# Fewer bias copies, two more pairs of PSUM banks at the start, and unit 1's weights made ready inside attention

## The chip, the core and the metric

The kernel runs on one core of a Trainium2 chip. The time is the device time of one execution, in microseconds (us). The engines are TensorE (PE; its weight loads are listed as PEld), VectorE (DVE), ScalarE (ACT), GpSimd (POOL) and SyncE (SP), which here only starts DMAs. Each engine runs its instructions strictly in the order in which they were written.

## The reference, cut to what matters

```
rel   = i - j                                           # S = 576 positions
x     = log1p(|rel|) / log1p(max(i, 1))
bias  = relu(x @ w1 + b1) @ w2                          # 1 -> 32 -> 8 heads
s     = q @ k.T / 8 + bias                              # B = 2, H = 8, D = 64
attn  = softmax(s);  a = attn @ v                       # a: 1152 tokens x 512
p     = domain_probs / sum(domain_probs)                # 4 experts
out   = sum over e of p[:, e] * (relu(a @ w1[e]) @ w2[e])   # 512 -> 1024 -> 512
```

## The kernel before, in words

**Bias rows.** The bias is the same for both batches, and its 576 x 576 x 8 values are made in 36 "rows" n. A row needs four features (L283 on ACT or L285 on DVE, into a ring `fr` of 8), eight fp32 matmuls (`bias_mm`, L290) into a pair of PSUM banks, and one copy out by ACT (`bias_out`, L293) into `obr`, a ring of three buffers. From there DMAs spread the row over the partitions of the table `biasA` or `biasB` (`bias_dma`): rows 0 to 3 with four DMAs of 144 KB each (L301), the others with two (L306). Rows 0 to 3 are block 0, rows 4 to 11 block 1, and so on in eights; the blocks alternate between the two tables.

**Attention.** There are 9 tiles of 128 tokens, and in each 4 pairs of heads. Scores for one head take 4 or 8 matmuls (L318) into a pair of banks of the same pool `b2` that the bias rows use; `b2` has two entries, banks 0 to 3. `ttr` (L326, DVE) adds the bias and takes the maximum; it needs every row of its block landed. Then follow exp (L330, ACT), transposes (L335, PE, into banks 4 to 7, pool `b1`), their eviction (L339 on ACT or L341 on DVE), attn @ v (L350, PE), the normalisation (L354 to L367), and the split of the result into two fp16 parts (`xhi` L377, `xlo` L380). `v_max` (L257) reads each of the eight loads of v for a common scale.

**Experts.** Each expert is two units of half its hidden width; unit u is half u % 2 of expert u // 2. The weights of a unit come in four loads of 512 KB (`load_w`, L421; m = 0 is w1, m = 1 is w2, j the half). They are brought to a common scale: `wmax` (L427) on each load, `w_both` (L436), a round trip through HBM that spreads the maximum over the partitions (`w_send` L439, `w_cast` L443, `w_red` L446), `pow2` (L267 to L271); then they are split in two fp16 parts (`whi` L457 or L459, `wlo` L463; for w1, `w_split` L577 on ACT and L578 on DVE into `wn`). Unit 0 is computed directly: `mm1` (L475 to L477), `ev_a` (L480, L481, ACT), `ev_v` (L484, DVE, `hh`), `mm2` (L497 to L499), and `sum_up` (L504, later L506) into `acc`. Units 1 to 7 compute their first product from sums of blocks in seven instead of eight products (`prod`, L594), which needs sums of x (`x_whole` L547 on POOL, `x_sums` L544, `x_halves` L553) and of weights (`w_sums`, L574, POOL).

**What sets the order.** A planner (class `Plan`) lists all operations with their dependencies, pools, modelled cost (`COST`) and priority (`PR`, `PEN`), and writes an order for each engine when the kernel is built. `plan` covers attention, unit 0 and its weights; `plan_experts`, a second planner, follows it and covers units 1 to 7 and the rest of unit 0. In the kernel before, unit 1's four weight loads are issued between the two planners, and everything else on these weights belongs to the second.

Of the kernel before, what the change touches and what calls it, by code (L numbers as in the profile page):

```python
# [155 lines left out]
def tile_attention_moe(ctx: ExitStack, tc: tile.TileContext, qd, kd, vd, cst, ltab, dp, mw1, mw2, out):  # L156
    nc = tc.nc
    V, A, G, T, SP = nc.vector, nc.scalar, nc.gpsimd, nc.tensor, nc.sync
    PR = CFG["PR"]
# [436 lines left out]
    def plan_experts():  # L596
# [13 lines left out]
        def weights(u):  # L610
            at = 42.0 * u - 34 if u > 1 else 5.0
            p2, p1 = u - 2, u - 1
            for m in range(2):
                for j in range(2):
                    if u > 1:
                        after = [("part", p1, k) for k in range(4)] if m == 0 else [("whi", p1, j), ("wlo", p1, j)]
                        op(("load", u, m, j), "S", at - 10, 1.4, lambda m=m, j=j: load_w(u, m, j), deps=after)
                    prev = ([("gate", p2)] + all_("part", p2, 4) + [("wlo", p2, k) for k in range(2)]) if p2 >= 1 else []
                    op(("wmax", u, m, j), "V", at + 2 * m + j, 1.21, lambda m=m, j=j: wmax(u, m, j), deps=[("load", u, m, j)] if u > 1 else [], after=prev)
                op(("wboth", u, m), "V", at + 2 * m + 2, 0.16, lambda m=m: w_both(u, m), deps=[("wmax", u, m, j) for j in range(2)], after=[("wred", u - 1)] if u > 1 else [])  # L620
            op(("wsend", u), "S", at + 4, 0.1, lambda: w_send(u), deps=[("wboth", u, m) for m in range(2)])
            op(("wcast", u), "S", at + 4, 0.5, lambda: w_cast(u), deps=[("wsend", u)])
            op(("wred", u), "V", at + 5, 0.45, lambda: w_red(u), deps=[("wcast", u)])
            for m in range(2):
                op(("wscale", u, m), "V", at + 6, 0.75, lambda m=m: wscale(u, m), deps=[("wred", u)])
            op(("wsum", u), "G", at + 8, 5.9, lambda: w_sums(u), deps=[("wmax", u, 0, j) for j in range(2)], after=[("part", p1, k) for k in range(4)] if u > 1 else [])
            used = [("prod", p2, i, q, k) for i in range(2) for q in range(2) for k in range(7)] if p2 >= 1 else []
            for k, (c, fns) in enumerate(zip((1.15, 0.63, 0.63, 1.6), w_parts(u))):
                for e, x, fn in zip("AV", (0, 0.15 * c), fns):
                    op((("parth" if e == "A" else "part"), u, k), e, at + 12 + 3 * k, c + x, fn, deps=[("wscale", u, 0)] + ([("wsum", u)] if k != 1 else []) + ([("parth", u, k)] if e == "V" else []), after=used)  # L630
            for j in range(2):
                used2 = [("mm2", p2, tau) for tau in range(NTAU)] if p2 >= 0 else []
                op(("whi", u, j), "A", 42.0 * u - 12 + 4 * j, 1.14, lambda j=j: whi("A", u, 1, j), deps=[("wscale", u, 1)], after=used2)
                op(("wlo", u, j), "V", 42.0 * u - 11 + 4 * j, 1.28, lambda j=j: wlo("V", u, 1, j), deps=[("whi", u, j)])
            op(("gate", u), "V", 42.0 * u - 4, 0.29, lambda: gate_unit(u), deps=[("wscale", u, m) for m in range(2)], after=[("sum", p2, tau) for tau in range(NTAU)] if p2 >= 0 else [])

        def second(u, tau, at):
            i = tau // 5
            if u:
                deps = [("lo", u, i, k) for k in range(8)] + [("wlo", u, j) for j in range(2)]  # L640
# [106 lines left out]
    for n in range(36):  # L747
# [66 lines left out]
    with tc.manual_schedule():  # L814
# [78 lines left out]
```

## Time and profile before

| | |
|---|---|
| median of 3 runs | 575.23 us (573.58 to 576.18) |
| the profiled execution, whole | 574.98 us |
| its span in the profile | 573.2 us |
| PE busy | 547.8 us, 96% |
| DVE busy | 407.9 us, 71% |
| ACT busy | 296.7 us, 52% |
| POOL busy | 139.7 us, 24% |
| HBM read | 25.75 MB |

PE is busy in nearly all of the span, so what an edit can give is read from the few stretches in which PE stands still or runs at the lower clock. Busy times count the modelled ends of pipelined matmuls; a busy PE may still wait for its input between instructions that overlap.

### The profile page before, as it was taken

The page shows a single profiled execution, that of the slowest core. Times are in us where ns is not written, and L with a number is a line of the kernel's source. Part 1 is how long each engine was busy: PE and PEld are TensorE (multiplying, and loading weights), DVE is VectorE, ACT ScalarE, POOL GpSimd, SP SyncE. Part 2 cuts the span into 40 slices and gives each one's busy share as a digit, 9 for nine tenths or more (in the row PEclk, how much of TensorE's full clock was granted, in tenths as well). Part 3 has the DMA queues.
Part 4 walks back from the last instruction along what each step waited for, and adds up shares of the span by engine and source line. Part 5 has one row for each costly group of instructions (what it writes and reads, how often), then busy time and mean ns, then how long its engine had stood idle before and what let it go on. Part 6 is the DMA issues. An engine that isn't in the chain of part 4 may idle for free.

```text
span 573.2 us, 11028 instructions
## 1 busy us (share of the span) xinstructions
PE 547.8 (96%) x4354; PEld 342.9 (60%) x4354; DVE 407.9 (71%) x827; ACT 296.7 (52%) x616; POOL 139.7 (24%) x153
## 2 busy tenths in 40 slices
PE   8469999999999999969999999999999999999997
PEld 3125767677777864526655665665665665565753
DVE  7348888887887468988596895986868858544532
ACT  5357887887788741454344633625525435423410
POOL 0000000000000045005427352362453534312310
PEclk9567999999999999998999999999999999999999
DMA  5585252324323000023140031311412200000022
GB/s 182 176 276 168 66 172 65 96 87 116 85 73 138 2 1 1 2 36 120 10 148 11 21 127 11 109 40 10 148 10 74 74 9 1 2 1 1 1 74 91
DMA packets 22020, 40.63 MB, mean 71 GB/s; under 512 B 3024, under 2 KB 4048, under 8 KB 21968
## 3 DMA queue, kind: packets, MB, share of 16 engines
q1 hardware_dynamic: 21680, 39.33, 23.4%
q8 instruction: 34, 0.56, 0.4%
q10 hardware_dynamic: 288, 0.59, 0.3%
q14 instruction: 18, 0.15, 0.1%
HBM read 25.75 MB, written 2.37 MB: 49 GB/s over the span
## 4 chain that ended last, share of the span: by engine, by line
PE 86%; DVE 4%; DMA 3%; ACT 3%; issue 1%; SPq 1%; POOL 1%; ACTq 0%; DVEq 0%; POOLq 0%
PE bank L594 24%; PE bank L499 10%; PE bank L497 10%; PE bank L498 10%; PE bank L350 7%; PE bank L318 7%; PE bank L335 7%; PE bank L290 5%; DVE hh L484 2%; PE bank L361 2%; DMA vv<-vd 1%; DMA biasB<-obr 1%; PE bank L230 1%; SPq L301 1%; DMA biasA<-obr 1%
## 5 line engine op out<-in xcount | busy, mean ns | idle before, releaser
L594 PEld LDWEIGHTS <-wn 128*128 128x128 f16 x1176 | 115.6, 99 | 47.6 <-DVE wn L578 4.3
L674 POOL TENSOR_TENSOR hp<-hf,hp 128x320 f16<-128x320 f32 (+1 forms) x112 | 89.9, 818 | 201.0 <-ACT hf L673 198.7
L672 ACT ACTIVATE hp<-xsf 128x320 f16<-128x320 f32 (+1 forms) x112 | 49.0, 437 | 131.7 <-DVE xsf L662 131.4
L594 PE MATMUL bank<-xs,wn 128*128 128x320 f16 (+1 forms) x672 | 99.8, 289 | 3.4 <-DVE wn L578 2.0
L662 DVE SCALAR_TENSOR_TENSOR xsf<-bank,xsf 128x320 f32<-128x320 f32 (+1 forms) x196 | 82.3, 451 | 24.0 <-PE bank L594 17.1
L506 DVE SCALAR_TENSOR_TENSOR acc<-bank,gu,acc 128x512 f32<-128x512 f32 x63 | 47.1, 748 | 68.1 <-PE bank L499 68.0
L594 PE MATMUL bank<-xx,wn 128*128 128x320 f16 (+1 forms) x504 | 76.5, 288 | 2.3 <-DVE wn L578 1.6
L285 DVE TENSOR_SCALAR fr<-lt,npt 128x576 f32<-128x576 f32 x115 | 52.3, 515 | 13.0 <-PE bank L290 12.9
L330 ACT ACTIVATE er<-er,mr 128x576 f32<-128x576 f32 x72 | 55.1, 770 | 8.3 <-DVE mr L326 8.2
L499 PE MATMUL bank<-wb,hp 128*128 128x512 f16 x144 | 54.6, 379 | 1.1 <-POOL hp L674 1.1
L290 PE MATMUL bank<-fr,cs 128*32 128x288 f32 x576 | 46.9, 453 | 8.2 <-ACT obr L293 5.6
L497 PE MATMUL bank<-wb,hp 128*128 128x512 f16 x144 | 54.6, 379 | 0.0
L498 PE MATMUL bank<-wb,hp 128*128 128x512 f16 x144 | 54.6, 379 | 0.0
L318 PE MATMUL bank<-ks,qr 64*128 64x288 f32 (+1 forms) x320 | 48.6, 452 | 4.7 <-ACT obr L293 4.7
L673 ACT ACTIVATE hf<-xsf 128x320 f32<-128x320 f32 (+1 forms) x112 | 47.8, 427 | 0.0
L339 ACT ACTIVATE etr<-bank 128x512 f32<-128x512 f32 x71 | 38.2, 598 | 16.6 <-PE bank L335 14.3
L350 PE MATMUL bank<-etr,vv 128*64 128x128 f32 (+1 forms) x800 | 45.2, 265 | 0.0
L350 PEld LDWEIGHTS bank<-etr,vv 128*64 128x64 f32 x800 | 39.8, 137 | 8.6 <-issue 5.5
L499 PEld LDWEIGHTS <-hp 128*128 128x128 f16 x252 | 24.7, 98 | 31.2 <-POOL hp L674 1.5
L326 DVE CUSTOM_DVE_ANT_0 er<-bank,biasA 128x576 f32<-128x576 f32 x40 | 28.8, 755 | 19.8 <-PE bank L318 19.0
L335 PE MATMUL bank<-ident,er 128*128 128x128 f32 x324 | 42.3, 281 | 0.0
L335 PEld LDWEIGHTS bank<-ident,er 128*128 128x128 f32 x324 | 35.6, 143 | 10.8 <-issue 8.5
(103 smaller groups left out, 772.5 us busy)
## 6 DMA issues: line engine op xcount, KB each, us to landing
raw<-mw SPq DMA_DIRECT2D x32, 512.0 KB
biasA<-obr SPq DMA_DIRECT2D x48, 144.0 KB
biasB<-obr SPq DMA_DIRECT2D x32, 144.0 KB
vv<-vd SPq DMA_DIRECT2D x8, 320.0 KB
ks<-kd SPq DMA_DIRECT2D x8, 288.0 KB
qr<-qd SPq DMA_DIRECT2D x9, 256.0 KB
out<-acc SPq DMA_DIRECT2D x8, 256.0 KB
wg<-wd SPq DMA_DIRECT2D x7, 128.0 KB
```

Source lines behind the costliest of these rows:

```text
L285: ENG[e].tensor_scalar(out=f, in0=src, scalar1=npt[:, g:g + 1], scalar2=None, op0=ALU.max)
L290: T.matmul(buf["pb", n][32 * t:32 * t + 32, half, 0:288], W2, buf["f", n, t][:, 288 * half:288 * half + 288], start=True, stop=True)
L318: T.matmul(s_out(2 * p + h, c0, c1, half), q[r, c0:c1], ks[r, HP * b + hp, 288 * half:288 * half + 288], start=True, stop=True)
L330: A.activation(out=ehalf(u), in_=ehalf(u), func=AF.Exp, scale=-1.0, bias=buf["m", u // 2][:, u % 2:u % 2 + 1], accum_out=buf["sum", tau][: ...
L335: T.transpose(buf["t", tau, g][:, P * i:P * i + P], buf["e", HP * tau + hp][:, P * j:P * j + P], ident)
L350: T.matmul(x[64 * h:64 * h + 64, P * hp + c0:P * hp + c1], vv[:, HP * b + hp, 5 * h + i], buf["et", tau, g][:, P * j + c0:P * j + c1], sta ...
L497: T.matmul(ps, hh[:, ft, ts], wh[:, ft], start=(ft == 0), stop=False)
L498: T.matmul(ps, hh[:, ft, ts], wl[:, ft], start=False, stop=False)
L499: T.matmul(ps, hl[:, ft, ts], wh[:, ft], start=False, stop=(ft == 3))
L594: T.matmul(ps, w[lw][:, k], x[:, lx, k], start=k == 0 and lw + lx == 0, stop=k == 1 and lw == 1)
L662: V.scalar_tensor_tensor(out=tmp(name), in0=ps(a), scalar=2.0 ** -HS, in1=tmp(other), op0=ALU.mult, op1=ALU.add)
L674: op(("lo", u, i, x), "G", at + pos + EV, 0.2 + 0.6 * r, lambda: G.tensor_tensor(out=lo, in0=buf[f][:, 0:n], in1=hi, op=ALU.subtract), dep ...
```

## The change

**Copies of rows 0 to 3.** Each row now goes out in two DMAs of 16 x 8 x 576 values, which read all 128 partitions of the `obr` buffer and write 64 partitions of `biasA`. The bytes are the same.

**Banks.** Rows 0, 1, 4, 5, 6 and 7 (`EARLY`) take their PSUM banks from a new pool `b2s`, two pairs in banks 4 to 7. These are the banks of the transposes, so the first group of transposes now waits for the copies out of these six rows.

**Unit 1's weights.** Loads, `wmax`, `w_both`, round trip, `pow2`, `whi`, `wlo` and `gate_unit` of unit 1 are operations of the first planner, so that they stand inside the last part of attention; the second planner keeps only `w_sums` and `w_split` for unit 1. A part of the loads waits for `wlo`, since it uses the same buffers.

**Order.** All priorities, and `SWITCH`, are new numbers; two of the lines stand here.

```diff
-    SWITCH=16.97,
+    SWITCH=19.41,
-        scores=-30.04, ttr=-262.39, exp=64.6, tr=17.92, evict=47.99, av=20.65, recip=49.21, rmat=11.82,
+        scores=-303.4, ttr=-915.8, exp=113.09, tr=4.03, evict=36.16, av=7.58, recip=-125.93, rmat=3.25,
...
+    pools["b2s"] = [bank[:, 4 + 2 * i:6 + 2 * i] for i in range(2)]
...
-            dst = bias[0].rearrange("(z v a r) (h s) -> z r v a h s", z=2, v=2, a=8, r=4, h=H)
+            dst = bias[0].rearrange("(z a r) (h s) -> z r a h s", z=2, a=16, r=4, h=H)
             for z in range(2):
-                for v in range(2):
-                    SP.dma_start(out=dst[z, n, v], in_=buf["o", n][64 * v:64 * v + 64])
+                SP.dma_start(out=dst[z, n], in_=buf["o", n])
...
+    EARLY = (0, 1, 4, 5, 6, 7)
...   # bias_mm
-    new=[("b2", ("pb", n))]
+    new=[("b2s" if n in EARLY else "b2", ("pb", n))]
...   # tr, first group
+    deps = ... + ([] if tau or g else [("bias_out", n) for n in EARLY])
...
+    early = PR["wprep"] + 60
+    for m in range(2):
+        for j in range(2):
+            free = [("wlo", 1, 0), ("wlo", 1, 1)] if m == 0 else []
+            op("load1", (m, j), early, load_first, m, j, after=[("open_b",)] + free, new=[] if m else [("wr", ("wr1", j))])
+            op("wmax1", (m, j), early, wmax, 1, m, j, deps=[("load1", m, j)], use=[] if m else [("wr1", j)])
+            if m:
+                op("whi1", (j,), early, whi, 1, m, j, choice=True, deps=[("wscale1", m)])
+                op("wlo1", (j,), early, wlo, "V", 1, m, j, deps=[("whi1", j)])
+        op("both1", (m,), early, w_both, 1, m, deps=[("wmax1", m, j) for j in range(2)])
+        op("wscale1", (m,), early, wscale, 1, m, deps=[("wred1",)])
+    op("wsend1", (), early, w_send, 1, deps=[("both1", 0), ("both1", 1)])
+    op("wcast1", (), early, w_cast, 1, deps=[("wsend1",)])
+    op("wred1", (), early, w_red, 1, deps=[("wcast1",)])
+    op("gate1", (), early, gate_unit, 1, deps=[("wscale1", 0), ("wscale1", 1), ("prep_gate",)])
...   # after plan.emit(buf)
-        for m in range(2):
-            for j in range(2):
-                load_w(1, m, j)
```

The line numbers in the pieces of the order below are those of the kernel each piece is from; those after are higher by 1 to 25. Eight L290 (L291 after) are one bias row, eight L318 the scores of two heads at the start, L335 transposes, L350 attn @ v. On PE, from the start, before:

```order
L290 MATMUL bank<-fr,cs 32x288 x64
L318 MATMUL bank<-ks,qr 64x288 x8
L290 MATMUL bank<-fr,cs 32x288 x16
L335 MATMUL bank<-ident,er 128x128 x8
L318 MATMUL bank<-ks,qr 64x288 x8
L290 MATMUL bank<-fr,cs 32x288 x8
L318 MATMUL bank<-ks,qr 64x288 x8
L335 MATMUL bank<-ident,er 128x128 x8
```

On PE, the same place, after:

```order
L291 MATMUL bank<-fr,cs 32x288 x40
L318 MATMUL bank<-ks,qr 64x288 x8
L291 MATMUL bank<-fr,cs 32x288 x40
L335 MATMUL bank<-ident,er 128x128 x8
L318 MATMUL bank<-ks,qr 64x288 x8
L291 MATMUL bank<-fr,cs 32x288 x16
L335 MATMUL bank<-ident,er 128x128 x8
L318 MATMUL bank<-ks,qr 64x288 x8
```

The first scores stand behind five bias rows instead of eight; ten rows still stand ahead of the first transposes.

On SP, the DMAs from the first bias copies (L301) on; ks, vv, qr are the loads of k, v and q. Before:

```order
L301 DMA biasA<-obr 8x8x576 x16
L250 DMA ks<-kd 128x576
L306 DMA biasB<-obr 8x8x576 x2
L250 DMA ks<-kd 128x576 x2
L306 DMA biasB<-obr 8x8x576 x2
L250 DMA ks<-kd 128x576
L306 DMA biasB<-obr 8x8x576 x2
L253 DMA vv<-vd 128x640
L306 DMA biasB<-obr 8x8x576 x2
L253 DMA vv<-vd 128x640 x6
L306 DMA biasB<-obr 8x8x576 x4
```

On SP, the same place, after:

```order
L301 DMA biasA<-obr 16x8x576 x8
L251 DMA ks<-kd 128x576
L306 DMA biasB<-obr 8x8x576 x2
L251 DMA ks<-kd 128x576 x2
L306 DMA biasB<-obr 8x8x576 x4
L251 DMA ks<-kd 128x576
L306 DMA biasB<-obr 8x8x576 x2
L254 DMA vv<-vd 128x640 x2
L306 DMA biasB<-obr 8x8x576 x4
L254 DMA vv<-vd 128x640 x6
L306 DMA biasB<-obr 8x8x576 x4
L275 DMA qr<-qd 128x512 x3
```

All sixteen copies of block 1 (L306 into `biasB`) now stand ahead of the second load of q; before, the last four of them stood behind the next two loads of q.

On DVE, after the last token tile of attention (`xlo`); hh is the second half of unit 0's first product, raw and raw_1679 are weight buffers. Before:

```order
L484 TENSOR_TENSOR hh<-hf,hh 128x384 x8
L504 TENSOR_SCALAR acc<-bank,gu 128x512
L427 TENSOR_REDUCE ws<-raw 128x1 x2
L504 TENSOR_SCALAR acc<-bank,gu 128x512
L544 TENSOR_TENSOR xsf<-xsf 128x2x320
L436 TENSOR_TENSOR wx<-ws 128x1
L544 TENSOR_TENSOR xsf<-xsf 128x2x320
L504 TENSOR_SCALAR acc<-bank,gu 128x512
L544 TENSOR_TENSOR xsf<-xsf 128x2x320
L427 TENSOR_REDUCE ws<-raw_1679 128x1
```

On DVE, the same place, after (from the third hh on):

```order
L484 TENSOR_TENSOR hh<-hf,hh 128x384
L459 TENSOR_SCALAR wb<-raw_1669,ws 128x1024
L463 SCALAR_TENSOR_TENSOR wb<-raw_1669,ws,wb 128x1024
L484 TENSOR_TENSOR hh<-hf,hh 128x384
L463 SCALAR_TENSOR_TENSOR wb<-raw_1669,ws,wb 128x1024
L484 TENSOR_TENSOR hh<-hf,hh 128x384 x4
L504 TENSOR_SCALAR acc<-bank,gu 128x512
L578 SCALAR_TENSOR_TENSOR wn<-raw,ws,wn 128x512
L427 TENSOR_REDUCE ws<-raw_1669 128x1
L504 TENSOR_SCALAR acc<-bank,gu 128x512
L544 TENSOR_TENSOR xsf<-xsf 128x2x320
```

Unit 1's wmax are gone from here (in after all four stand ahead of the last `xlo`), its `whi` and `wlo` stand between the first hh, and a wmax of unit 2 has come in.

## Rows read from the trace of the kernel before

**Rows 1.** The page's 40 equal slices of the span: PE busy, and its clock, in tenths.

```profile
PE   8469999999999999969999999999999999999997
PEclk9567999999999999998999999999999999999999
```

**Rows 2.** Waits, 0 to 60 us: who waited for whom, us in total, times, longest.

```profile
ACT obr L293 <- DMA biasA<-obr: 9.3, 4, 3.1
PE bank L290 <- ACT obr L293: 5.6, 3, 2.6
PE bank L318 <- ACT obr L293: 4.7, 3, 2.4
```

**Rows 3.** ACT's timeline: start, us, operation, [idle before <- releaser].

```profile
27.96 0.74 ACT L293 ACTIVATE obr<-bank,cs 128x576 f32<-128x576 f32 x1 [3.12 <-DMA biasA<-obr]
...
31.36 0.74 ACT L293 ACTIVATE obr<-bank,cs 128x576 f32<-128x576 f32 x1 [2.00 <-DMA biasB<-obr]
```

**Rows 4.** PE's timeline, same columns, 32 to 58 us.

```profile
32.15 2.19 PE L318 MATMUL bank<-ks,qr 64*64 64x288 f32 x12 [2.17 <-ACT obr L293]
...
54.42 2.15 PE L290 MATMUL bank<-fr,cs 128*32 128x288 f32 x32
...
57.81 1.24 PE L318 MATMUL bank<-ks,qr 64*128 64x288 f32 x8
```

**Rows 5.** DVE's timeline: the first `ttr`, and the first one of block 1.

```profile
33.56 0.76 DVE L326 CUSTOM_DVE_ANT_0 er<-bank,biasA 128x576 f32<-128x576 f32 x1 [5.78 <-PE bank L318]
...
59.18 0.76 DVE L326 CUSTOM_DVE_ANT_0 er<-bank,biasB 128x576 f32<-128x576 f32 x1 [0.87 <-PE bank L318]
```

**Rows 6.** Stretches: busy of PE, PEld, DVE, ACT, POOL, then clock, DMA share, GB/s.

```profile
4.00:8.00 4.00, 4.00 (x18) 1.34 (x18) 3.79 (x16) 1.89 (x3) 0.00 (x0) 1.00 0.99 364
...
12.00:24.00 12.00, 6.64 (x60) 2.00 (x58) 5.24 (x13) 5.82 (x9) 0.00 (x0) 0.71 0.51 158
24.00:46.00 22.00, 14.46 (x118) 5.77 (x120) 10.85 (x24) 11.38 (x21) 0.00 (x0) 0.66 0.87 259
...
60.00:200.00 140.00, 140.00 (x1693) 103.95 (x1692) 111.00 (x276) 112.53 (x234) 3.42 (x4) 1.00 0.30 90
...
251.00:263.00 12.00, 7.32 (x32) 3.51 (x30) 10.15 (x13) 6.40 (x9) 0.79 (x1) 0.72 0.52 172
...
150.00:200.00 50.00, 50.00 (x572) 39.14 (x572) 35.49 (x90) 38.69 (x82) 0.68 (x1) 1.00 0.23 73
```

**Rows 7.** PE's timeline where unit 1's products begin.

```profile
252.15 0.45 PE L594 MATMUL bank<-xx,wn 128*128 128x320 f16 x2 [0.69 <-ACT wn L577]
...
257.76 1.25 PE L594 MATMUL bank<-xs,wn 128*128 128x320 f16 x4 [2.04 <-DVE wn L578]
```

**Rows 8.** SP's timeline (SPq is its DMA queue): DMAs issued, first 60 us.

```profile
9.56 13.54 SPq L301 DMA_DIRECT2D biasA<-obr  x16
...
43.14 1.13 SPq L274 DMA_DIRECT2D qr<-qd  x2
45.13 8.01 SPq L306 DMA_DIRECT2D biasB<-obr  x4
```

**Rows 9.** Groups of DVE instructions, 205.5 to 260 us: busy us, mean ns.

```profile
L504 DVE TENSOR_SCALAR acc<-bank,gu 128x512 f32<-128x512 f32 x9 | 6.7, 747 | 3.6 <-PE bank L499 3.6
L427 DVE TENSOR_REDUCE ws<-raw 128x1 f32<-128x1024 f32 x5 | 6.0, 1208 | 0.0
```

**Rows 10.** `whi` on DVE, whole span: ns min/median/max, when.

```profile
L459 DVE TENSOR_SCALAR wa<-raw,ws x1: 750/750/750, 120.1 to 120.1; 128x1024 f16<-128x1024 f32 x1
```

**Rows 11.** DVE's timeline, unit 0's second half and unit 2's first load.

```profile
209.02 11.71 DVE L484 TENSOR_TENSOR hh<-hf,hh 128x384 f16<-128x384 f32 x6 [1.02 <-ACT hh L481]
...
259.01 1.21 DVE L427 TENSOR_REDUCE ws<-raw 128x1 f32<-128x1024 f32 x1
```

**Rows 12.** POOL's timeline at the same time as the hh.

```profile
207.86 9.37 POOL L547 TENSOR_TENSOR xsf<-xx 128x2560 f32<-128x2560 f16 x2 [48.12 <-DVE xx L380]
```

**Rows 13.** SP's timeline: unit 2's loads.

```profile
255.34 3.96 SPq L421 DMA_DIRECT2D raw<-mw  x4
```

More of the change, by code (lines that the diff above doesn't have):

```diff
@@ L612, in weights @@
             p2, p1 = u - 2, u - 1
-            for m in range(2):
+            for m in range(2 if u > 1 else 0):
                 for j in range(2):
                     if u > 1:
-                        after = [("part", p1, k) for k in range(4)] if m == 0 else [("whi", p1, j), ("wlo", p1, j)]
+                        after = [("part", p1, k) for k in range(4)] if m == 0 else [("whi", p1, j), ("wlo", p1, j)] if p1 > 1 else []
                         op(("load", u, m, j), "S", at - 10, 1.4, lambda m=m, j=j: load_w(u, m, j), deps=after)
-                    prev = ([("gate", p2)] + all_("part", p2, 4) + [("wlo", p2, k) for k in range(2)]) if p2 >= 1 else []
+                    prev = (all_("part", p2, 4) + ([("gate", p2)] + [("wlo", p2, k) for k in range(2)] if p2 > 1 else [])) if p2 >= 1 else []
@@ L623, in weights @@
[L623 to L626, printed above, removed]
+                op(("wboth", u, m), "V", at + 2 * m + 2, 0.16, lambda m=m: w_both(u, m), deps=[("wmax", u, m, j) for j in range(2)], after=[("wred", u - 1)] if u > 2 else [])
@@ new lines, in weights @@
+            if u > 1:
+                op(("wsend", u), "S", at + 4, 0.1, lambda: w_send(u), deps=[("wboth", u, m) for m in range(2)])
+                op(("wcast", u), "S", at + 4, 0.5, lambda: w_cast(u), deps=[("wsend", u)])
+                op(("wred", u), "V", at + 5, 0.45, lambda: w_red(u), deps=[("wcast", u)])
+                for m in range(2):
+                    op(("wscale", u, m), "V", at + 6, 0.75, lambda m=m: wscale(u, m), deps=[("wred", u)])
+            op(("wsum", u), "G", at + 8, 5.9, lambda: w_sums(u), deps=[("wmax", u, 0, j) for j in range(2)] if u > 1 else [], after=[("part", p1, k) for k in range(4)] if u > 1 else [])
@@ L639, in second @@
             if u:
-                deps = [("lo", u, i, k) for k in range(8)] + [("wlo", u, j) for j in range(2)]
+                deps = [("lo", u, i, k) for k in range(8)] + ([("wlo", u, j) for j in range(2)] if u > 1 else [])
             else:
@@ L643, in second @@
             op(("mm2", u, tau), "T", at, 2.6, lambda: mm2(u, tau, buf["o", u, tau]), deps=deps, new=[("o", ("o", u, tau))])
-            op(("sum", u, tau), "V", at + 2.6 + EV, 0.75, lambda: sum_up(u, tau, buf["o", u, tau]), deps=[("mm2", u, tau)] + ([("gate", u)] if u else []), use=[("o", u, tau)], after=[("sum", u - 1, tau)] if u else [])
+            op(("sum", u, tau), "V", at + 2.6 + EV, 0.75, lambda: sum_up(u, tau, buf["o", u, tau]), deps=[("mm2", u, tau)] + ([("gate", u)] if u > 1 else []), use=[("o", u, tau)], after=[("sum", u - 1, tau)] if u else [])
             if u == NU - 1:
@@ L726, in plan_experts @@
         return plan
+    EARLY = (0, 1, 4, 5, 6, 7)
+    KIND = {"load1": "load_w", "wmax1": "wmax", "whi1": "whi", "wlo1": "wlo", "both1": "wmax_both", "wscale1": "wscale", "wsend1": "wsend", "wcast1": "wcast", "wred1": "wred", "gate1": "gate_unit"}
     def op(kind, key, prio, fn, *args, choice=False, **kw):
-        plan.add((kind,) + key, kind, prio, (lambda e: fn(e, *args)) if choice else (lambda e: fn(*args)), **kw)
+        name, kind = kind, KIND.get(kind, kind)
+        plan.add((name,) + key, kind, prio, (lambda e: fn(e, *args)) if choice else (lambda e: fn(*args)), **kw)
     def chain(kind, u):
@@ L755, in tile_attention_moe @@
         old = [("ttr", 16 * (block - 2) + 7)] if block > 1 else []
-        op("bias_mm", (n,), base + PR["bias_mm"], bias_mm, n, deps=[("feat", n, t) for t in range(4)], after=chain("bias_mm", n) + (old if (n - 4) % 8 >= 3 else []) + ([("scores", (n - 8) // 2 if n < 12 else n - 10)] if n >= 8 else []), new=[("b2", ("pb", n))], use=[("f", n, t) for t in range(4)], mode="col4")
+        op("bias_mm", (n,), base + PR["bias_mm"], bias_mm, n, deps=[("feat", n, t) for t in range(4)], after=chain("bias_mm", n) + (old if (n - 4) % 8 >= 3 else []) + ([("scores", (n - 8) // 2 if n < 12 else n - 10)] if n >= 8 else []), new=[("b2s" if n in EARLY else "b2", ("pb", n))], use=[("f", n, t) for t in range(4)], mode="col4")
         op("bias_out", (n,), base + PR["bias_out"], bias_out, n, deps=[("bias_mm", n)], after=chain("bias_out", n), new=[("ob", ("o", n))], use=[("pb", n)])
-        op("bias_dma", (n,), base + PR["bias_dma"], bias_dma, n, deps=[("bias_out", n)] + old, after=chain("bias_dma", n), use=[("o", n)], cost=COST["bias_dma8" if n < 4 else "bias_dma"])
+        op("bias_dma", (n,), base + PR["bias_dma"], bias_dma, n, deps=[("bias_out", n)] + old, after=chain("bias_dma", n), use=[("o", n)], cost=COST["bias_dma4" if n < 4 else "bias_dma"])
     for tau in range(NTAU):
@@ L776, in tile_attention_moe @@
             at = 2 * ps[-1] + (4 * g + 3) % 9 * 0.1
-            op("tr", (tau, g), at + PR["tr"], tr, tau, g, deps=[("exp", 2 * p + h) for p in ps for h in range(2)], after=[("tr", tau, g - 1)] if g else [("tr", tau - 1, 8)] if tau else [], new=[("b1", ("t", tau, g))], use=[("e", p) for p in ps])
+            op("tr", (tau, g), at + PR["tr"], tr, tau, g, deps=[("exp", 2 * p + h) for p in ps for h in range(2)] + ([] if tau or g else [("bias_out", n) for n in EARLY]), after=[("tr", tau, g - 1)] if g else [("tr", tau - 1, 8)] if tau else [], new=[("b1", ("t", tau, g))], use=[("e", p) for p in ps])
             op("evict", (tau, g), at + PR["evict"], evict, tau, g, choice=True, deps=[("tr", tau, g)], new=[("et", ("et", tau, g))], use=[("t", tau, g)], after=[("evict", tau, g - 1)] if g else [("evict", tau - 1, 8)] if tau else [])
@@ L801, in tile_attention_moe, with load_first @@
     op("gate_unit", (), PR["wprep"] + 22, gate_unit, 0, deps=[("wscale", 0), ("wscale", 1), ("prep_gate",)])
-    hold = {}
+    def load_first(m, j):
+        if m == 0:
+            moe["raw"][j] = buf["wr1", j]
+        load_w(1, m, j)
+    early = PR["wprep"] + 60
+    for m in range(2):
+        for j in range(2):
[11 more added lines that the diff above has]
+    op("gate1", (), early, gate_unit, 1, deps=[("wscale1", 0), ("wscale1", 1), ("prep_gate",)])
     for c in range(2):
```

24 lines of the change are left out of this document (11 added, 13 removed).

## The prediction

> **What bounds the kernel now.** I read the slices first, to find where PE is not busy. The reader is to see only two weak places before the end: the second and third slice of 14.3 us (14 to 43 us) and the eighteenth (244 to 258 us), with the clock's digits low there or just behind [rows 1]. Everywhere else PE has no idle time, so only work taken from PE could help there, and the change takes none.
>
> For the start I read the waits next. ACT's copy of a bias row into `obr` waited 9.3 us for earlier copies to leave that ring, and PE waited 5.6 + 4.7 = 10.3 us for ACT [rows 2]. It is one chain: the DMA out of `obr` is late, so ACT cannot empty the banks, so PE cannot write the next row or the first scores, because both use the same two pairs of banks. The timelines show where it ends: ACT writes a row at 27.96 only when a copy of block 0 has landed, and another at 31.36 when one of block 1 has [rows 3]; the scores follow at 32.15 [rows 4], and the first `ttr` comes at 33.56, after 5.78 us of waiting for them [rows 5]. From block 1's first `ttr` on, at 59.18 [rows 5], PE is never idle: 140 of 140 us [rows 6]. So 59.18 is the mark: what the start gains is how much earlier this `ttr` runs.
>
> Why are the copies slow? In 12 to 24 us, when they are nearly all that moves, the DMA engines are busy for 0.51 and move 158 GB/s; in 4 to 8 us, when the loads run, it is 0.99 and 364 GB/s [rows 6]. These copies keep half of the engines busy.
>
> [...]
>
> **The change part by part.** The sum is made against the profiled execution, 574.98 us, which lies 0.25 below the median.
>
> *Start, first copies.* 16 DMAs of 144 KB become 8 of 288 KB; the bytes (2.36 MB) stay. Before, they are issued from 9.56 [rows 8] and done at 27.96, 18.4 us. If the same engines carry them, nothing changes. If all engines do, as in the loads, the rate doubles and the copies end at 9.56 + 9.2 = 18.8. A `ttr` follows at least 0.7 us later (one L293), which makes 19.5 for the first one; at the old rate it comes at about 27.9. Nothing in the trace shows a copy that reads 128 partitions and writes 64, so I take the middle, 23.7, and keep both ends.
>
> [...]
>
> *Start, banks and order.* Scores need five rows now instead of eight, and two of them free the pair, so PE no longer waits for `obr` before the first `ttr`; the wait goes to the copies' landing. The new wait of the first transposes costs nothing: in the order ten bias rows stand ahead of them in both kernels, and ACT writes eight rows before its first exp in both.
>
> *Start, what is late next.* Between the first `ttr` and block 1's first, the queue has to carry (from the order's shapes, 4 bytes each) four loads of k (1152 KB), sixteen copies of block 1 (2304 KB), eight loads of v (2560 KB) and one of q (256 KB): 6.42 MB. In 24 to 46 us the same mix ran at 259 GB/s with the engines busy for 0.87 [rows 6]. So 24.8 us: 23.7 + 24.8 = 48.5, and with one round of scores, 1.24 us [rows 4], block 1's `ttr` at 49.7 instead of 59.2. That is 9.5 earlier, less one bias row that by the order PE then has still to do. The trace has 16 records for a row's eight matmuls, so the 32 in 2.15 us are two rows [rows 4], and one is 1.0: 8.5 stay. With the ends of the first copies, 19.5 gives 12.7 and 27.9 gives 4.2. The last part of this gain rests on SP's order: before, block 1's last four copies stood behind two more loads of q and went out at 45.13 [rows 8]; now they stand ahead of these.
>
> *Attention.* Four `wmax` of 1.21 us [rows 9] and small operations come in, 5.5 us, into a stretch where DVE is busy for 35.5 of 50 us while PE is busy for all of it [rows 6]. PE's queue covers them unless one stands right ahead of a `ttr` that the next scores' banks wait for: at worst 1.2 us each. I take a loss of 0.5 (range 0 to 1.5), all in the last tile, where little is queued ahead of PE.
>
> *Transition to unit 1.* The ceiling is 12 - 7.32 = 4.68 us of idle PE and the low clock: 7.32 x (1 - 0.72) = 2.05; together 6.7. The engine waited for is DVE, busy for 10.15 of 12 [rows 6], so I count what it does before the last `wn`. Gone: four `wmax`, 4 x 1.21 = 4.8, and three sums into `acc` that now come after the last `wn`, 3 x 0.75 = 2.2 [rows 9]. New: one `whi` of 0.75 [rows 10], which was ACT's, and two `wmax` of unit 2, 2.4. Net 3.9 earlier. Against it: `whi` and `wlo` now stand between the hh, which `mm2` needs. Before, six hh took 11.71 instead of 6 x 0.55 [rows 11] because POOL's sums of x ran at the same time for 9.37 us [rows 12]: a DVE operation of this kind waits until POOL's ends. Two more such operations in this stretch can cost from nothing to the 4 us that one held hh takes. It helps that PE has 7 us of `mm1` left there. I take 4.0 from the ceiling's 6.7 (range 0 to 6.7): the net of DVE's count, and PE's clock stays up if the gap nearly closes.
>
> Sum: 574.98 - 8.5 - 4.0 + 0.5 = 563.0.
>
> **Rivals.**
>
> *R1, the copies stay at their rate.* The start gains 4.2: the banks and the order still let the first `ttr` start at the landing, 27.9 instead of 33.56. 574.98 - 4.2 - 4 + 0.5 = 567.3. [...] Chance 0.2.
>
> *R2, the transition gives nothing.* POOL's long operations hold DVE's new `whi` and `wlo`, the hh and so `mm2` come later, and what DVE saved is given back. 574.98 - 8.5 + 0.5 = 567. For it: the 11.71 for six hh. Against: three of the four `wn` parts need nothing but POOL's sums and DVE. [...] Chance 0.12.
>
> *R3, slower: unit 1's weights hold up attention.* DVE runs in order, so a `wmax` whose load has not landed stops every `ttr` behind it. A load takes 259.01 - 255.34 = 3.7 us from issue to its `wmax` [rows 13, 11], and SP can issue the two w1 loads only when `wlo` of unit 0 has freed the buffers. Four such waits, each with its `wmax` of 1.2, are 19.6 us. DVE has 14.5 of 50 us free there [rows 6], but free time elsewhere doesn't help a wait that comes all at once. If each is exposed in full: 574.98 - 8.5 - 4 + 19.6 = 582. It decides from 12.5 us exposed; 15.4 are needed for a time 0.5% longer. Against: between the last `wlo` and the first `wmax` of a load that waits for it the order has a pair of `ttr`; 35 pairs in the 140 us of [rows 6] are 4.0 us for one, about a load's 3.7. Chance 0.06.
>
> *R4, the start's wait only moves.* The last copies of block 1 wait in SP's queue for `obr` as before, and the second q comes behind them; block 1's `ttr` runs at 58. Start gain 1: 570.5. For it: SP issued the last four at 45.13 to 53.14 [rows 8], slowly. Against: what made them slow was the loads of q ahead and the `obr` ring behind, and both move up. Chance 0.04.
>
> **How the numbers follow.** Forecast 0.58, R1 0.2, R2 0.12, R3 0.06, R4 0.04. The likeliest gives 563.0, with its own range 557 to 567: 12.7 + 6.7 at best gives 555.6, and half of the start's gain lost gives 567. R1 and R2 lie at its upper edge, both together at 571; with R4 inside as well, 553 to 571 leaves out R3 and a start better than the doubled rate. A measurement here tells 0.5%, 2.9 us, from no change. Faster by more than that are the forecast, R1, R2 and R4, less a tail where several go wrong at once: 0.87; the same 0.07; slower 0.06 (R3).
>
> **What would show it.** First copies: the DMA share and GB/s while they run alone; near 1.0 and 300 GB/s for doubling, 0.51 and 158 for R1. First `ttr`: 19.5, 23.7 or 27.9. Block 1's first `ttr` near 50, and no idle PE behind it; at 58, R4. Transition: the idle time before the first L594 and the wait for DVE `wn` gone, and the clock of 251 to 263 us (moved by the gain) at 1.0; hh of more than 2 us with a `wlo` beside POOL, for R2. Attention: in the waits, DVE L427 for the DMA of `raw`; more than a few us is R3. The forecast is wrong if the mark at block 1 moves by less than 4 us, or if PE shows a new gap between there and the end of attention.

## The result

The changed kernel takes 566.44 us in the median (566.17 to 566.97, 4 runs) beside 575.69 us for the kernel before (573.58 to 576.18, 4 runs): a ratio of 0.9867, 95% interval 0.9839 to 0.9894, which is faster by 1.3%. The forecast was 563.0 us with a range of 553 to 571. The profiled span fell from 573.2 to 564.4 us, by 8.8.

The page's slices of the changed kernel, PE's busy tenths and its clock, against [rows 1]:

```profile
PE   8769999999999995999999999999999999999997
PEclk9799999999999997999999999999999999999999
```

Two things are to be seen. The second slice went from 4 to 7 and the clock there from 5 to 7. And the weak slice between attention and the experts has not gone: it is the sixteenth (5, with a clock of 7) instead of the eighteenth (6). A slice is 14.1 us long here, so it lies at 212 to 226 us.

### The start

The waits of 0 to 60 us, changed kernel (who waited for whom: us in total, times, longest); they answer to [rows 2]:

```profile
ACT obr L294 <- DMA biasA<-obr: 4.3, 3, 2.7
...
PE bank L291 <- ACT obr L294: 3.2, 2, 2.9
...
PE bank L318 <- ACT obr L294: 2.4, 3, 1.4
```

PE waited 10.3 us for the copies out of its banks; now it is 3.2 + 2.4 = 5.6. DVE's timeline (start, us, operation, [idle before <- releaser]) has the two marks of [rows 5], the first `ttr` and block 1's first:

```profile
22.96 0.76 DVE L326 CUSTOM_DVE_ANT_0 er<-bank,biasA 128x576 f32<-128x576 f32 x1 [3.03 <-DMA biasB<-obr]
...
49.41 0.76 DVE L326 CUSTOM_DVE_ANT_0 er<-bank,biasB 128x576 f32<-128x576 f32 x1 [1.11 <-PE bank L318]
```

The first `ttr` comes 10.6 us earlier and now waits for a DMA, not for PE. The row names a copy into `biasB`, which this `ttr` does not need by the program; just before it the last copies of block 0 landed, for which ACT's seventh row was waiting:

```profile
22.89 0.74 ACT L294 ACTIVATE obr<-bank,cs 128x576 f32<-128x576 f32 x1 [0.46 <-DMA biasA<-obr]
```

The first copies, issued from 9.54, thus took 13.4 us instead of 18.4. Block 1's first `ttr` comes 9.77 us earlier. The stretches (length, busy us of PE, PEld, DVE, ACT, POOL, clock, DMA share, GB/s) answer to [rows 6]:

```profile
12.00:18.00 6.00, 5.40 (x64) 2.00 (x64) 3.79 (x10) 4.23 (x7) 0.00 (x0) 1.00 1.06 241
...
12.00:24.00 12.00, 8.49 (x95) 3.01 (x94) 6.69 (x16) 7.09 (x11) 0.00 (x0) 0.88 1.05 249
24.00:46.00 22.00, 17.35 (x194) 8.88 (x193) 14.92 (x33) 14.72 (x29) 0.00 (x0) 0.91 0.82 263
...
60.00:190.00 130.00, 130.00 (x1529) 94.84 (x1527) 108.67 (x260) 103.72 (x214) 5.49 (x6) 1.00 0.31 95
```

In 12 to 24 us, while the first copies run, the DMA share is 1.05 instead of 0.51 and the rate 249 GB/s instead of 158; in 12 to 18 us, where they run nearly alone (the next load of k is issued at 16.35), it is 1.06 and 241. A copy now reads 128 partitions of `obr` where it read 64. What it writes, by the `rearrange` in the diff, is not 64 partitions of `biasA` but 16, every fourth of 64, where it was 8, every fourth of 32. In the stretch of 60 to 190 us PE is busy for 130.00 of 130.00 us, so unit 1's loads and `wmax` fit there.

### The transition

DVE's last L367 marks the end of attention; the first row is the kernel before, the second the changed one.

```profile
205.66 0.69 DVE L367 TENSOR_TENSOR xf<-bank,rs 128x512 f32<-128x512 f32 x1 [3.52 <-PE bank L350]
```

```profile
197.13 0.69 DVE L367 TENSOR_TENSOR xf<-bank,rs 128x512 f32<-128x512 f32 x1 [3.55 <-PE bank L350]
```

Attention ends 8.53 us earlier. Unit 1's products then begin without any gap behind the last `mm2`; PE's timeline of the changed kernel, with its first L594 and the nineteenth, against [rows 7]; the nineteenth follows three groups of six. Ahead of them stands the one gap that PE has in this stretch:

```profile
218.39 0.59 PE L497 MATMUL bank<-wa,hh 128*128 128x512 f16 x1 [6.67 <-ACT hh L481]
...
251.50 0.98 PE L594 MATMUL bank<-xx,wn 128*128 128x320 f16 x6
...
253.94 1.79 PE L594 MATMUL bank<-xs,wn 128*128 128x320 f16 x12
```

These are PE's waits in the kernel before, 200 to 300 us:

```profile
PE bank L594 <- DVE wn L578: 3.6, 2, 2.0
PE bank L594 <- ACT wn L577: 1.1, 2, 0.7
PE bank L499 <- POOL hp L674: 1.1, 1, 1.1
PE bank L497 <- ACT hh L481: 0.4, 1, 0.4
```

The four waits for `wn`, 4.68 us in total, are gone, but `mm2`, which waited 0.4 us, now waits 6.67 us in one piece. The clock is 1.00 in 210 to 215 us, falls within the gap, is 0.50 in 216 to 222 and 1.00 again from 223 on, some 4 us behind the gap's end:

```profile
215.00:220.00 5.00, 1.61 (x4) 0.56 (x4) 3.87 (x5) 2.14 (x5) 0.82 (x1) 0.56 0.52 177
220.00:225.00 5.00, 5.00 (x19) 2.06 (x18) 1.82 (x3) 0.00 (x0) 0.00 (x0) 0.75 0.01 5
```

At 0.56 and 0.75 of full speed, 1.61 and 5.00 us of busy PE lose 0.7 + 1.25 = 2.0 us, by an estimate from these two rows. In the kernel before, the nineteenth product matmul (behind groups of 2, 4, 2, 4 and 6) was at

```profile
260.40 2.07 PE L594 MATMUL bank<-xs,wn 128*128 128x320 f16 x7
```

The balance is therefore: block 1's mark 9.77 earlier; from there to L367 147.72 instead of 146.48, 1.24 lost (one bias row more that PE has still to do, and the rest); L367 to the nineteenth product 56.81 instead of 54.74, 2.07 lost; from there to the end of the span 310.44 instead of 312.80, 2.36 won. Sum: -8.8. The 2.36 have two main sources. The kernel before still ran at the lower clock, 0.50 from 256 to 262 us, when it reached its nineteenth product: at 0.87 in 260 to 270 us, 10.00 us of busy PE lose 1.3 by the same kind of estimate, some 1.1 of it behind that product. Its wait of 1.1 us for POOL's `hp`, in the list above, is not in the changed kernel either. This is the stretch in the kernel before:

```profile
260.00:270.00 10.00, 10.00 (x66) 6.71 (x65) 7.78 (x16) 4.41 (x12) 5.13 (x6) 0.87 0.30 110
```

What held `mm2` is to be read from three engines, changed kernel. ACT waited for DVE's hh before it could empty the next bank of the first product:

```profile
214.79 0.49 ACT L480 ACTIVATE hf<-bank 128x384 f32<-128x384 f32 x1 [4.55 <-DVE hh L484]
...
217.47 0.49 ACT L480 ACTIVATE hf<-bank 128x384 f32<-128x384 f32 x1 [1.80 <-DVE hh L484]
```

Many of DVE's operations were slow at that time, first an hh, then `gate_unit`, `whi` and `wlo`; not all were, as the first row of `pow2`, of 0.14 us, shows:

```profile
200.96 3.91 DVE L484 TENSOR_TENSOR hh<-hf,hh 128x384 f16<-128x384 f32 x1 [0.24 <-ACT hh L481]
...
204.79 0.14 DVE L268 TENSOR_SCALAR ws<-ws 128x1 f32<-128x1 f32 x1
...
205.60 3.22 DVE L452 TENSOR_SCALAR gu<-gate,ws 128x9 f32<-128x9 f32 x1
...
209.20 1.75 DVE L459 TENSOR_SCALAR wb<-raw,ws 128x1024 f16<-128x1024 f32 x1
210.88 2.29 DVE L463 SCALAR_TENSOR_TENSOR wb<-raw,ws,wb 128x1024 f16<-128x1024 f32 x1
...
214.62 2.28 DVE L463 SCALAR_TENSOR_TENSOR wb<-raw,ws,wb 128x1024 f16<-128x1024 f32 x1
```

And POOL was in its sums all the while:

```profile
199.32 9.47 POOL L547 TENSOR_TENSOR xsf<-xx 128x2560 f32<-128x2560 f16 x2 [9.91 <-DVE xx L380]
...
212.04 3.78 POOL L574 TENSOR_TENSOR wt<-raw,wt 128x512 f32<-128x512 f32 x2
```

With POOL idle, in the run with POOL late below, an hh takes 0.56 us, `gate_unit` 0.29, `whi` 0.75 and a `wlo` 1.28; here they take up to 3.91, 3.22, 1.75 and 2.29. The first two of these ended with POOL's sums of x: the hh at 204.87 and `gate_unit` at 208.82, the two sums at 204.45 and 208.79. In the kernel before, the first two of the six hh [rows 11] ended at 213.30 and 217.64, its two sums [rows 12] at 212.90 and 217.23.

### The profile page after: what moved, and what is told of

It reads as the page before. It is cut to its first block, busy times and chain, and to the rows that moved or that the text cites. A ratio compares the mean times of both kernels' runs of the same rounds, so it can differ in the third digit from the quotient of the medians.

```text
span 564.4 us, 11030 instructions
## 1 busy us (share of the span) xinstructions
PE 542.4 (96%) x4354; PEld 341.4 (60%) x4354; DVE 408.4 (72%) x829; ACT 293.8 (52%) x611; POOL 146.3 (26%) x156
## 4 chain that ended last, share of the span: by engine, by line
PE 87%; DVE 5%; DMA 4%; ACT 2%; issue 1%; SPq 0%; ACTq 0%; DVEq 0%
PE bank L594 24%; PE bank L497 11%; PE bank L499 11%; PE bank L498 11%; PE bank L350 7%; PE bank L318 7%; PE bank L335 7%; PE bank L291 5%; PE bank L361 2%; DMA biasA<-obr 1%; DMA biasB<-obr 1%; DVE hh L484 1%; DMA vv<-vd 1%; DVE wb L463 1%; PE bank L231 1%
## 5 line engine op out<-in xcount | busy, mean ns | idle before, releaser
L677 POOL TENSOR_TENSOR hp<-hf,hp 128x320 f16<-128x320 f32 (+1 forms) x112 | 92.1, 838 | 203.4 <-ACT hf L676 202.4
L594 PEld LDWEIGHTS <-wn 128*128 128x128 f16 x1176 | 115.0, 98 | 40.4 <-issue 1.7
L665 DVE SCALAR_TENSOR_TENSOR xsf<-bank,xsf 128x320 f32<-128x320 f32 (+1 forms) x196 | 82.4, 451 | 25.6 <-PE bank L594 18.4
L594 PE MATMUL bank<-xs,wn 128*128 128x320 f16 (+1 forms) x672 | 98.2, 286 | 1.0 <-ACT xsf L685 0.6
L594 PE MATMUL bank<-xx,wn 128*128 128x320 f16 (+1 forms) x504 | 75.5, 286 | 0.0
L330 ACT ACTIVATE er<-er,mr 128x576 f32<-128x576 f32 x72 | 55.2, 769 | 10.6 <-DVE mr L326 10.4
L318 PE MATMUL bank<-ks,qr 64*128 64x288 f32 (+1 forms) x320 | 47.2, 427 | 5.1 <-ACT obr L294 2.4
L291 PE MATMUL bank<-fr,cs 128*32 128x288 f32 x576 | 44.4, 434 | 3.8 <-ACT obr L294 3.2
L350 PE MATMUL bank<-etr,vv 128*64 128x128 f32 (+1 forms) x800 | 45.5, 265 | 0.0
L350 PEld LDWEIGHTS bank<-etr,vv 128*64 128x64 f32 x800 | 39.6, 137 | 8.6 <-issue 6.8
L335 PE MATMUL bank<-ident,er 128*128 128x128 f32 x324 | 42.1, 278 | 0.0
L335 PEld LDWEIGHTS bank<-ident,er 128*128 128x128 f32 x324 | 34.8, 141 | 12.0 <-issue 8.4
L497 PE MATMUL bank<-wa,hp 128*128 128x512 f16 x108 | 40.9, 379 | 0.0
```

What stands on the lines that cost most here:

```text
L291: T.matmul(buf["pb", n][32 * t:32 * t + 32, half, 0:288], W2, buf["f", n, t][:, 288 * half:288 * half + 288], start=True, stop=True)
L318: T.matmul(s_out(2 * p + h, c0, c1, half), q[r, c0:c1], ks[r, HP * b + hp, 288 * half:288 * half + 288], start=True, stop=True)
L330: A.activation(out=ehalf(u), in_=ehalf(u), func=AF.Exp, scale=-1.0, bias=buf["m", u // 2][:, u % 2:u % 2 + 1], accum_out=buf["sum", tau][: ...
L335: T.transpose(buf["t", tau, g][:, P * i:P * i + P], buf["e", HP * tau + hp][:, P * j:P * j + P], ident)
L350: T.matmul(x[64 * h:64 * h + 64, P * hp + c0:P * hp + c1], vv[:, HP * b + hp, 5 * h + i], buf["et", tau, g][:, P * j + c0:P * j + c1], sta ...
L497: T.matmul(ps, hh[:, ft, ts], wh[:, ft], start=(ft == 0), stop=False)
```

## The experiments

The ratios are to the kernel before, run beside each on the same chip, with their 95% intervals.

### Unit 1's whi and wlo behind the hh

```diff
-op("whi1", (j,), ..., deps=[("wscale1", m)])
+op("whi1", (j,), ..., deps=[("wscale1", m)], after=[("ev_v", 1, 3)])
-op("gate1", (), ..., deps=[..., ("prep_gate",)])
+op("gate1", (), ..., deps=[..., ("prep_gate",)], after=[("ev_v", 1, 3)])
```

> Changed kernel, but unit 1's gate_unit, whi and wlo wait for the last hh of unit 0's first two thirds, so that they stand behind the hh instead of between them (the planner then puts whi on ACT). Theory A (the operations that were put between the hh make the second product late): the 6.67 us in which PE stood before mm2 shrink to 0.4 to 1.5 us, as in the kernel before (0.41), the lower clock behind them goes (about 2 us), and unit 1's products still start without a gap: 558 to 561 us. Theory B (POOL's sums hold up the hh whatever stands between them): the gap stays at 4 us or more, 563 to 566 us.

Measured: 559.34 us, ratio 0.9734 (0.9709 to 0.9759), some 7 us below the changed kernel. PE's gap, and the six hh that now follow each other on DVE:

```profile
213.71 0.38 PE L497 MATMUL bank<-wa,hh 128*128 128x512 f16 x1 [1.58 <-ACT hh L481]
```

```profile
205.90 10.35 DVE L484 TENSOR_TENSOR hh<-hf,hh 128x384 f16<-128x384 f32 x6
```

Theory A gave the time; the gap, 1.58, is a little over its range. The hh are still held by POOL, 10.35 us for six beside 11.71 in [rows 11], but six held hh alone cost `mm2` 1.58 us and not 6.67.

### POOL's sums of x behind the hh

```diff
 def x_whole(i):
+    if i == 0:
+        G.tensor_copy(out=moe["wt"][:, 0:1], in_=hpart(0, 1, 1)[:, 3, 383:384])
     G.tensor_tensor(out=moe["xf"][:, :, tokens(i)], in0=xx[:, 0, :, tokens(i)], ...)
```

> Changed kernel, but POOL's sums of x wait for the last hh (a one-column copy on POOL reads it first), so that POOL is idle while the hh, whi and wlo run. Theory B (POOL's operations hold DVE's): each hh takes 0.55 us instead of up to 3.9, gate_unit 0.3 instead of 3.2, wlo 1.3 instead of 2.3, and the gap before mm2 is 1 us or less; what POOL now does 10 us later may stop DVE at the sums of x or at wn, so 558 to 566 us. Theory A (it is the number of operations between the hh): the operations are as many, and the gap stays at 3 us or more.

Measured: 559.23 us, ratio 0.9741 (0.9710 to 0.9772). The order on DVE is that of the changed kernel, `whi` and `wlo` between the hh; its timeline, PE's and POOL's:

```profile
202.02 0.29 DVE L452 TENSOR_SCALAR gu<-gate,ws 128x9 f32<-128x9 f32 x1
202.67 0.56 DVE L484 TENSOR_TENSOR hh<-hf,hh 128x384 f16<-128x384 f32 x1 [0.36 <-ACT hh L481]
203.15 0.75 DVE L459 TENSOR_SCALAR wb<-raw,ws 128x1024 f16<-128x1024 f32 x1
203.81 1.28 DVE L463 SCALAR_TENSOR_TENSOR wb<-raw,ws,wb 128x1024 f16<-128x1024 f32 x1
```

```profile
212.44 0.38 PE L497 MATMUL bank<-wa,hh 128*128 128x512 f16 x1 [0.96 <-ACT hh L481]
```

```profile
213.34 9.50 POOL L549 TENSOR_TENSOR xsf<-xx 128x2560 f32<-128x2560 f16 x2
```

Theory B holds: with POOL idle an hh takes 0.56 us and `gate_unit` 0.29, and the gap goes from 6.67 us to 0.96. Either edit takes most of the stall away, so neither theory is the whole of it: the operations between the hh cost `mm2` 6.67 us only because POOL held them, and POOL's hold reached `mm2` only because there was more to hold.

### Both at once

The diffs of the two, together.

> Changed kernel with both edits of the transition: gate_unit, whi and wlo behind the hh, and POOL's sums of x behind the last hh. If each edit alone removed the same stall (the operations between the hh cost much only while POOL holds DVE), both together gain no more than the rest of the gap before mm2, 0.5 to 1 us: 558 to 559.5 us. If they removed different stalls, the gains add up: 555 us or less.

Measured: 564.67 us, ratio 0.9827 (0.9791 to 0.9864): 5 us slower than either alone, which neither expectation gave. The two `wlo` (1.28 us each in the run above) now began just behind POOL's sums; DVE, then POOL:

```profile
216.38 11.00 DVE L463 SCALAR_TENSOR_TENSOR wb<-raw,ws,wb 128x1024 f16<-128x1024 f32 x2 [0.27 <-ACT wb L457]
```

```profile
216.26 10.04 POOL L549 TENSOR_TENSOR xsf<-xx 128x2560 f32<-128x2560 f16 x2
```

The hold is the same and has moved: 11.00 us for 2.6 us of work, and the sums into `acc`, the sums of x and `wn` come late behind it; of the 70 us from 190 to 260 PE was busy for 65.77. This is the clearest picture of the hold in the study. Part of the loss lies elsewhere: in this profile block 1's first `ttr` ran at 50.77, 1.4 later than in the changed kernel with the same program up to there, and attention ended at 199.8 instead of 197.1. The profile is of the slowest of this kernel's four runs (562.47 to 566.71 us), so how the 5 us divide stays open.

### The copies alone

```diff
-dst = bias[0].rearrange("(z v a r) (h s) -> z r v a h s", z=2, v=2, a=8, r=4, h=H)
+dst = bias[0].rearrange("(z a r) (h s) -> z r a h s", z=2, a=16, r=4, h=H)
 for z in range(2):
-    for v in range(2):
-        SP.dma_start(out=dst[z, n, v], in_=buf["o", n][64 * v:64 * v + 64])
+    SP.dma_start(out=dst[z, n], in_=buf["o", n])
```

> Kernel before with one edit: rows 0 to 3 go out in two DMAs of 128 partitions read, not four of 64; orders and banks as before. Theory C (the copies' rate sets the start): first ttr at about 27 us instead of 33.6, block 1's first at 54 to 56 instead of 59.2, time 570 to 572 us. Rival D (without the new order and banks the copies give nothing, because the last copies of block 1 stand behind loads of q): block 1's first ttr at 58 or later, 574 us or more.

Measured: 570.21 us, ratio 0.9924 (0.9895 to 0.9952). The two marks, and 12 to 24 us:

```profile
27.18 0.76 DVE L325 CUSTOM_DVE_ANT_0 er<-bank,biasA 128x576 f32<-128x576 f32 x1 [3.52 <-issue]
...
55.25 0.76 DVE L325 CUSTOM_DVE_ANT_0 er<-bank,biasB 128x576 f32<-128x576 f32 x1 [0.87 <-PE bank L317]
```

```profile
12.00:24.00 12.00, 7.24 (x80) 2.45 (x72) 6.86 (x15) 7.85 (x12) 0.00 (x0) 0.83 1.05 247
```

Theory C, in all its numbers: the copies alone move block 1's mark by 3.9 of the 9.8 us. The copy's outer size and the number of partitions that it reads both double, and no run here changes one without the other, so which of the two raises the DMA share from 0.51 to 1.05 is not shown.

### Four copies in the changed kernel

The same diff the other way round, in the changed kernel.

> Changed kernel with one edit undone: rows 0 to 3 go out in four DMAs again; orders and banks are those of the changed kernel. Theory C: DMA share 0.5 in 12 to 24 us, first ttr at about 28 us instead of 23.0, block 1's first at 53 to 54 instead of 49.4, time 570 to 571 us. Rival D (order and banks carry the gain): block 1's first ttr within 1.5 us of 49.4, time 566 to 568 us.

Measured: 572.09 us, ratio 0.9963 (0.9946 to 0.9980). The marks, and 12 to 24 us:

```profile
26.13 0.76 DVE L327 CUSTOM_DVE_ANT_0 er<-bank,biasA 128x576 f32<-128x576 f32 x1 [3.68 <-DMA ks<-kd]
...
54.89 0.76 DVE L327 CUSTOM_DVE_ANT_0 er<-bank,biasB 128x576 f32<-128x576 f32 x1 [1.63 <-PE bank L319]
```

```profile
12.00:24.00 12.00, 7.05 (x84) 2.64 (x80) 5.58 (x13) 5.90 (x9) 0.00 (x0) 0.96 0.53 176
```

Theory C again, but the mark and the time lie outside its ranges, the mark 0.9 us later than the latest that it gave: without the copies the change loses 5.5 us there. Banks and order without the copies give 4.3 of the 9.8, and the copies alone gave 3.9; together they give 1.6 more than the sum.

### Four copies that read all partitions

```diff
 for z in range(2):
-    SP.dma_start(out=dst[z, n], in_=buf["o", n])
+    for g in range(2):
+        SP.dma_start(out=dst[z, n][:, :, 288 * g:288 * g + 288], in_=buf["o", n][:, 288 * g:288 * g + 288])
```

> Changed kernel; rows 0 to 3 go out in four DMAs each again, but every one reads all 128 partitions and half of each one's 576 values (16 x 8 x 288 instead of 8 x 8 x 576). Bytes as before, as many DMAs on SP as in the kernel before. Theory F (the outer size of 16 puts the copies on all engines, and that is the gain): DMA share near 1.0 in 12 to 24 us, block 1's first ttr at 49 to 51 us, time 566 to 568 us. Theory G (SP's time to issue 16 DMAs, 0.5 to 0.8 us each, is what the four copies per row cost): share near 0.5, block 1's first ttr at 53 to 55 us, about 571 to 572 us.

Measured: 569.21 us, ratio 0.9902 (0.9873 to 0.9931). The marks, 12 to 24 us, and SP's first copies of block 1 (in the changed kernel they are issued at 17.71, with four copies of 64 partitions at 22.98):

```profile
23.51 0.76 DVE L327 CUSTOM_DVE_ANT_0 er<-bank,biasA 128x576 f32<-128x576 f32 x1 [2.70 <-DMA biasA<-obr]
...
53.51 0.76 DVE L327 CUSTOM_DVE_ANT_0 er<-bank,biasB 128x576 f32<-128x576 f32 x1 [0.46 <-PE bank L319]
```

```profile
12.00:24.00 12.00, 7.41 (x92) 2.65 (x84) 6.07 (x14) 6.46 (x10) 0.00 (x0) 0.97 0.75 207
```

```profile
9.46 11.53 SPq L302 DMA_DIRECT2D biasA<-obr  x16
...
21.72 1.43 SPq L307 DMA_DIRECT2D biasB<-obr  x2
```

It lies between the theories, and the two marks tell them apart. The first `ttr` is early (23.51, theory F): with 16 in the outer size, and 128 partitions read, it comes 0.55 us later than in the changed kernel, where four copies of 64 partitions made it 3.2 us later. Block 1's mark is late (53.51, theory G): SP took 11.53 us to issue sixteen copies, against 6.77 us for eight in the changed kernel, and the first copies of block 1 behind them went out 4.0 us later. That SP and not the data was late is seen at the fourth row, which ACT wrote at 14.35 in the changed kernel and at 14.37 here: its copies are the last of the first copies, and SP had issued these by 16.31 there (9.54 + 6.77) and by 20.99 here (9.46 + 11.53). The runs of bytes are half as long in this experiment, and the share is 0.75, so it does not show how much of the 4.1 us at the mark is the issue alone.

### One pool of banks

```diff
-new=[("b2s" if n in EARLY else "b2", ("pb", n))]
+new=[("b2", ("pb", n))]
-deps=[("exp", ...) ...] + ([] if tau or g else [("bias_out", n) for n in EARLY])
+deps=[("exp", ...) ...]
```

> Changed kernel without the two extra pairs of banks (all bias rows take the two pairs of before, and the first transposes have no wait for six rows); the planner then puts eight rows ahead of the first scores again, and the last four copies of block 1 behind loads of q. Theory E (banks and the order that they allow carry the part of the start's gain that the copies alone didn't give): block 1's first ttr at 54 to 56 us, like that of the copies alone (55.3), time 570 to 573 us. Rival: the new priorities and the copies do it all: block 1's first ttr before 51.5 us, 566 to 568 us.

Measured: 560.84 us, ratio 0.9761 (0.9738 to 0.9783): some 6 us faster than the changed kernel, where 4 to 7 slower was expected. The mark, and 190 to 260 us:

```profile
53.22 0.76 DVE L326 CUSTOM_DVE_ANT_0 er<-bank,biasB 128x576 f32<-128x576 f32 x1 [0.86 <-PE bank L318]
```

```profile
190.00:260.00 70.00, 70.00 (x501) 44.01 (x497) 59.30 (x87) 33.23 (x65) 24.32 (x14) 1.00 0.12 33
```

At the start the theory stands, nearly: without the banks the mark comes 3.8 us later, 0.8 short of the range. But the planner, given fewer banks, wrote another order up to the end of attention as well, and there the gap is gone. Seven hh are left behind attention instead of eight, and 75 matmuls of the first product ahead of `mm2` instead of 90. The hold itself is still there:

```profile
206.69 4.25 DVE L484 TENSOR_TENSOR hh<-hf,hh 128x384 f16<-128x384 f32 x1
```

So this run doesn't price the banks; it shows that the gap of 6.67 us belongs to one order and not to the preparation of unit 1 as such. The two runs that change only the copies of the changed kernel (four copies, and four that read all partitions) have the same gap, 6.67 us in each.

## Why the prediction was right in its time and wrong in one step

**The start** (forecast 8.5) was right in size, and in its mechanism in the main. From the first `ttr` to block 1's took 26.45 us, where the sum of bytes had 24.8 and one round of scores, 26.0. With the loss in attention, the end of attention was to come 8.0 us earlier and came 8.53 earlier. That the first `ttr`, put at 23.7, came at 22.96 is luck: 23.7 was the middle of two ends, the old rate and the doubled one, and neither came. The DMA share did double, from 0.51 to 1.05, but the rate rose from 158 to 249 GB/s only. The share is a mean: it does not tell whether half of the engines carried the copies before, as the prediction reads it, or more of them for a part of the time. Nor was the division seen rightly: the prediction had the copies' rate as the only price of the four copies. The runs show the rate (share 1.05 instead of 0.53, first `ttr` 3.2 us earlier) and, beside it, that with sixteen copies to issue the first copies of block 1 go out 4.0 us later. R1 is out by the share of 1.05 and the 249 GB/s. R4 (mark at 58) is out as well, and so is R3: PE was busy for 130 of 130 us in 60 to 190 us. That DVE runs in the written order, from which R3 starts, both traces show: its 827 and 829 instructions stand in them as in the programs.

**Attention** (forecast a loss of 0.5) was right: 1.24 between the marks, of which the prediction had set down 1.0 as the bias row that is still to do; 0.24 are left, within its range of 0 to 1.5.

**The transition** (forecast 4.0) is the step that failed: "I take 4.0 from the ceiling's 6.7 (range 0 to 6.7): the net of DVE's count, and PE's clock stays up if the gap nearly closes." The ceiling is read from 251 to 263 us of the kernel before [rows 6], where unit 1's products waited for `wn` [rows 7]. The stretch and what follows it gave 2.36 - 2.07 = 0.3. The count of DVE's work ahead of `wn` was right in its direction, and the gap before unit 1's products closed wholly. What failed is the price of the operations put between the hh. It had been named for two of them, "from nothing to the 4 us that one held hh takes", and then set at nothing; the only ground given is that PE had 7 us of `mm1` left. It cost 6.67 us of idle PE and some 2.0 of clock, more than the bound. Not one operation was held but a row of them, one after the other, and four of them were new: `gate_unit`, which the prediction left out of its count and which was held longest, `whi` and two `wlo` took 9.5 us, against 3.6 in the run with POOL late. Each hh stood behind the one before through ACT's ring. That is rival R2 in mechanism, place and time (567 forecast, 566.44 measured), and its chance of 0.12 was too low for the evidence that the trace of before had: 11.71 us for six hh of 0.55 [rows 11], and POOL busy for nearly all of that time [rows 12]. The prediction quoted both and set the price at nothing. The time lay in the stated range because the range had been made wide enough for R1 and R2; the forecast itself was 3.4 us off.

Two edits show the price by experiment: without the operations between the hh, or without POOL beside them, the kernel runs in 559.3 and 559.2 us and beats both.

## What to carry to other kernels

Before work is moved into a stretch, ask what runs on POOL there. Here an hh of 0.56 us lasted 3.91 beside POOL's sums and a `gate_unit` of 0.29 us 3.22, `whi` and `wlo` were held too, and the single-column operations of `pow2`, of 0.14 to 0.16 us, were not, so look in a trace which of yours are. Price a row of them by the held duration, not by their own. When a wait of several microseconds is removed, follow the engine that it set free to its next stop; here the gap moved some 31 us ahead, counted from the end of attention, from `wn` to `mm2`, and grew from 4.68 to 6.67 us. And count what a DMA costs its issuer: eight first copies were issued in 6.77 us, sixteen in 11.53 and 12.51, and with eight the copies of block 1 went out 4.0 and 5.3 us earlier.

## What the hardware showed that was not expected

`gate_unit`, a DVE operation on 128 x 9 values, took 3.22 us beside POOL's sums and 0.29 without them, while the five operations of `pow2` on 128 x 1 took 0.14 to 0.16 each beside the same sums. Two `wlo` took 11.00 us beside two POOL operations of 10.04 together, and 1.28 each without. Copies from SBUF to SBUF moved 241 GB/s at a DMA share of 1.06 (12 to 18 us), where loads moved 367 at 0.97:

```profile
4.00:8.00 4.00, 4.00 (x18) 1.47 (x18) 3.81 (x16) 1.91 (x3) 0.00 (x0) 1.00 0.97 367
```
